# A fused attention and gated expert kernel: first h phase through the out-projection's banks, and a new order of early loads

## The chip, the cores and the metric

The kernel runs on one core of a Trainium2 chip. The metric is device time in microseconds for one execution, lower is better; the median over repeated runs is compared.

## The reference

Two stages are chained. The first attends twice in each of 8 batches and 8 heads, with 576 positions, head size 64 and 32 packed queries p:

```python
def sm_attn(qq, kk, vv):
    s = scale * np.matmul(qq, kk.transpose(0, 1, 3, 2))
    s = s - np.max(s, axis=-1, keepdims=True)
    a = np.exp(s)
    a = a / (np.sum(a, axis=-1, keepdims=True) + 1e-09)
    return np.matmul(a, vv)
p_packed = sm_attn(p, k, v)
out = sm_attn(q, p_packed, p_packed)
```

The second takes the result as 4608 tokens of 512 and computes, with 2048 inner columns:

```python
h = x @ w_in
g = h * np.cos(h)
return (g @ w_out).astype(np.float32)
```

Inputs and the output are float32.

## The kernel before, in words

Everything on chip is bfloat16 with float32 accumulation. The work goes batch by batch, each in these steps:

- `load` (L81) brings k, v or q of a batch from HBM and casts it on the way; it is a DMA issued by POOL (GpSimd). `load_w_in` and `load_w_out` bring each of the two weights in four blocks of 512 KB, also from POOL's queue.
- k and q are transposed, on TensorE (`pe_T`, L94, three groups of eight transposes, each group copied out of PSUM) or by a DMA transpose issued by SP (`xbar`, L90). v is rearranged by a copy, `permute_v` (L85), on DVE (VectorE) or POOL.
- `s1` (L128): scores of the packed queries against k, exponentials on ACT (ScalarE). The exponentials are transposed by `a1_pe` (TensorE) or `a1_xbar` (DMA). `pp` (L157) multiplies them with v and lays the result out as `ppT`.
- `ppw` (L174): instead of multiplying attention's output with w_in, the packed values are multiplied with w_in first, in four pieces n of 512 columns, giving `PPW`. Each piece is copied out of PSUM by DVE or ACT.
- `s2` (L185), `sums2` and `normalise`: scores of q against the packed values, exponentials, sums by a matmul with ones, a logarithm and a negative exponential on ACT, and the product `a2n` on DVE.
- h phase, 16 chunks `fc` of 128 inner columns: `h_mm` (L212) makes h in PSUM by four matmuls (L220), the cosine on ACT (L224), and the product `gT` on DVE (L227). Every eight chunks POOL copies the last 64 rows into `joint`, where two batches share one output chunk.
- out-projection: `out_gen` (L265) yields after each of 16 matmuls (L270) per chunk of 128 rows, then copies the result to `osb`, alternately by DVE and ACT, and writes it out from SP.

The order is written by hand: engines run their own instructions in program order. The out-projection of the previous batch is the filler: `fill(n)` (L287) puts n of its matmuls at the place where it stands, so that TensorE has work while another engine is waited for. `slot` (L394) runs an h phase with the remaining fillers spread over its chunks, and with inserted work at named chunks. `warm` puts dummy matmuls at the start. In the loop from L426 on, each batch has the same sequence: second attention of batch s, first attention of batch s+1 and DMA transposes for s+1, then the h phase of s.

PSUM is in two pools: `psA`, three tiles of two banks each (`psa`, L78), used by the h phase and by all attention steps, and `psO`, two single banks (`ot`), used by the out-projection and by the dummy matmuls. An h chunk holds its `psA` tile until DVE has made the product.

POOL's loads run in the order of issue. A small POOL copy into `gate` makes POOL wait for a DMA transpose before it issues the loads behind it. The ACT tables for exponentials and for the cosine are different; each change is a table load.

The first h phase (L356 to L361) has no filler, since no previous batch exists. After it come the first attention of batch 1 with the first batch's out-projection between its steps, then batch 2's first attention, and the h phase of batch 1 as a slot.

Of the kernel before, what the change touches and what calls it, by code (L numbers as in the profile page):

```python
# [8 lines left out]
FP32 = mybir.dt.float32  # L9
BF16 = mybir.dt.bfloat16  # L10
# [5 lines left out]
def kernel(  # L16
# [55 lines left out]
    def copy(eng, out, in_):  # L72
        if eng is ACT:
            ACT.copy(out=out, in_=in_)  # L74
        else:
            eng.tensor_copy(out=out, in_=in_)  # L76

    def psa(dt=FP32):  # L78
        return A.tile([128, 2, 512 if dt == FP32 else 1024], dt, name="psA", tag="A")

    def load(n, b):  # L81
        bf[n, b] = bf_pool.tile([TP, H, C * D], BF16, name=n + "bf", tag=n + "bf")
        G.dma_start(out=bf[n, b], in_=srcs[n][b].rearrange("h (p c) d -> p h (c d)", c=C))  # L83

    def permute_v(b, eng=G):  # L85
# [2 lines left out]
             bf["v", b].rearrange("p h (c d) -> p c h d", c=C))  # L88

    def xbar(n, b):  # L90
        t = xT[n, b] = att_pool.tile([128, H * 3, TP], BF16, name=n + "T", tag=n + "T")
        nc.sync.dma_start_transpose(out=t, in_=bf[n, b].rearrange("p h x -> p (h x)"))

    def pe_T(n, b, engs=(V, V, V)):  # L94
        t = xT[n, b] = att_pool.tile([128, H * 3, TP], BF16, name=n + "T", tag=n + "T")
        flat = bf[n, b].rearrange("p h x -> p (h x)")
        for i in range(3):
            ps = psa(BF16)
            for j in range(8):
                o = 8 * i + j  # L100
                nc.tensor.transpose(ps[:, 0, j * TP:(j + 1) * TP], flat[:, o * 128:(o + 1) * 128],  # L101
                                    ident[0:TP, 0:TP])
            copy(engs[i], t[:, 8 * i:8 * i + 8].rearrange("p a x -> p (a x)"),
                 ps[:, 0, 0:8 * TP])

    def pack_p(b0, b1):
        ng = 2 * (b1 - b0)
        ps = psa(BF16)
        flat = ps.rearrange("p a x -> p (a x)")
        for g in range(ng):  # L110
            nc.tensor.transpose(flat[:, g * 128:(g + 1) * 128],
                                p_bf[:, 2 * b0 + g].rearrange("p t d -> p (t d)"), ident)
        V.tensor_copy(out=P2[:, b0:b1].rearrange("p b h n -> p (b h n)"), in_=flat[:, 0:ng * 128])
# [32 lines left out]
        nc.sync.dma_start_transpose(out=t.rearrange("p a c x -> p (a c) x"),  # L146
                                    in_=a1[b % 2].rearrange("p a c x -> p (a c x)"))

    def a1_pe(b):
        t = a1T[b] = att_pool.tile([128, 2, C, 128], BF16, name="a1T", tag="a1T")  # L150
        for y in range(2):
            ps = psa(BF16)
            for c in range(C):
                nc.tensor.transpose(ps[0:TP, 0, c * 128:(c + 1) * 128], a1[b % 2][:, y, c, 0:TP], ident)
            copy(V, t[0:TP, y].rearrange("p c x -> p (c x)"), ps[0:TP, 0, 0:C * 128])
# [15 lines left out]
            z = slice(64 - 64 * y, 128 - 64 * y)  # L171
            ACT.copy(out=t[z, :, y, :], in_=pv[r, :, y, :])  # L172

    def ppw(b, n, eng=None):  # L174
        if b not in PPW:
            PPW[b] = ppw_pool.tile([128, 2, DF], BF16, name="PPW", tag="PPW")
        ps = psa()
        for x in range(4):
            for y in range(2):
                r = slice(64 * y, 64 * y + 64)  # L180
                nc.tensor.matmul(ps[32 * x:32 * x + 32, y, :], ppT[b % 2][r, 2 * x + y, :],  # L181
                                 w_in_bf[r, x, n * 512:(n + 1) * 512], start=True, stop=True)
        copy(eng or (V, ACT)[n % 2], PPW[b][:, :, n * 512:(n + 1) * 512], ps)

    def s2(b):  # L185
        a2u[b] = att_pool.tile([128, 2, S], BF16, name="a2u", tag="a2u")
# [63 lines left out]
    def n_chunks(b):  # L250
        return 5 if b % 2 and b < B - 1 else 4
# [11 lines left out]
                q.dma_start(out=rows[:, cols], in_=osb[a:z, cols])  # L263

    def out_gen(b):  # L265
        for c in range(n_chunks(b)):
            ps = O.tile([128, DM], FP32, name="ot", tag="ot")
            for fc in range(NFC):
                w = joint[b // 2][:, fc, :] if c == 4 else gT[b][:, fc, c * 128:(c + 1) * 128]
                nc.tensor.matmul(ps, w, w_out_bf[:, fc, :], start=(fc == 0), stop=(fc == NFC - 1))  # L270
                if fc < NFC - 1:
                    yield
            osb = o_pool.tile([128, DM], FP32, name="osb")
            copy((V, ACT)[n_out[0] % 2], osb, ps)
            n_out[0] += 1
            for a, z, rows in pieces_of(b, c):
                nc.sync.dma_start(out=rows, in_=osb[a:z, :])
            yield

    filler = [None, 0]  # L280

# [11 lines left out]
    def load_w_in(n):  # L293
        G.dma_start(out=w_in_bf[:, :, n * 512:(n + 1) * 512],
                    in_=moe_w_in.rearrange("(a p) n -> p a n", p=128)[:, :, n * 512:(n + 1) * 512])

    def load_w_out(n):
        G.dma_start(out=w_out_bf[:, n * 4:(n + 1) * 4, :],
                    in_=moe_w_out.rearrange("(a p) n -> p a n", p=128)[:, n * 4:(n + 1) * 4, :])

    def dup_p(a, b):
        for t in range(2):
            V.tensor_copy(out=p_bf[:, a:b, t, :], in_=p_raw[:, a:b, :])

    def warm(n):
        for _ in range(n):
            nc.tensor.matmul(wps, wz[:, 0:128], wz, start=True, stop=True)

# [2 lines left out]
    load("v", 0)  # L311
    make_identity(nc, ident)
    load("q", 0)
    load_w_in(0)
    load_w_in(1)
    G.dma_start(out=p_raw[:, 2:, :], in_=p_rows[:, 2:, :])
    load_w_in(2)
    load_w_in(3)
    for n in range(4):
        load_w_out(n)  # L320
    load("k", 1)
    load("v", 1)
    load("q", 1)
    load("k", 2)
    load("v", 2)
    load("q", 2)
    wz = const.tile([128, 512], BF16, name="wz")
    wps = O.tile([128, 512], FP32, name="wps", tag="ot")
    V.memset(wz, 0.0)
    ACT.preload_act_table_set(EXP_SET)  # L330
    V.memset(ones_blk, 0.0)
# [3 lines left out]
        V.memset(t[:, :, :, TP:128], 0.0)  # L335

    warm(7)
    dup_p(0, 2)
    pack_p(0, 1)
    warm(9)  # L340
    pe_T("k", 0, (V, ACT, V))
    s1(0)
    permute_v(0, V)
    warm(3)
    a1_pe(0)
    recips(0)
    pp(0)
    pe_T("q", 0, (V, ACT, V))
    s2(0)
    ppw(0, 0)  # L350
    sums2(0, 0)
    sums2(0, 1)
    normalise(0)
    warm(6)
    dup_p(2, 16)
    for fc in range(NFC):  # L356
        h_mm(0, fc)()
        if fc in (1, 4, 7):
            ppw(0, 1 + fc // 3)
        if fc == 10:  # L360
            pack_p(1, 3)  # L361

    set_filler(0)
    ACT.preload_act_table_set(EXP_SET)
    fill(4)
    pe_T("k", 1)
    fill(3)
    s1(1)
    permute_v(1, V)
    fill(8)  # L370
    a1_pe(1)
    recips(1)
    fill(4)
    pp(1)
    pe_T("q", 1)
    fill(3)
    ppw(1, 0)
    s2(1)
    fill(4)
    pe_T("k", 2)  # L380
    ppw(1, 1)
    fill(3)
    s1(2)
    fill(4)
    sums2(1, 0)
    fill(4)
    sums2(1, 1)
    normalise(1)
    fill(6)
    a1_pe(2)  # L390
    recips(2)
    load("k", 3)

    def slot(s, pieces, hooks, keep=5):  # L394
        left = filler[1] - keep
        for fc in range(NFC):
            rest = h_mm(s, fc)
            while pieces and pieces[0][0] == fc:
                pieces.pop(0)[1]()
            rest()  # L400
            while hooks and hooks[0][0] == fc:
                hooks.pop(0)[1]()
            done = left + keep - filler[1]
            fill((left * (fc + 1)) // NFC - done)

    def pw(b, n):
        return lambda: ppw(b, n)

    def pw2(b):
        fill(4)  # L410
        ppw(b, 0)
        ppw(b, 1)
        fill(4)

    def begin_loads(b):
        G.tensor_copy(out=gate, in_=xT["k", b][0:1, 0, 0:1])
        for n, i in (("v", b), ("q", b), ("k", b + 1)):
            load(n, i)

    permute_v(2)  # L420
    xbar("q", 2)
    xbar("k", 3)
    slot(1, [(1, pw(1, 2)), (4, pw(1, 3)), (7, lambda: pp(2)), (9, lambda: pack_p(3, B)),
             ], [(8, lambda: begin_loads(3)), (12, lambda: pw2(2))])

    for s in range(2, B):  # L426
        nxt = s + 1 < B
        fill(1000)
        set_filler(s - 1)
        ACT.preload_act_table_set(EXP_SET)  # L430
        if nxt:
            permute_v(s + 1)
        s2(s)
        ppw(s, 2, V)
        fill(8)
        if nxt:
            s1(s + 1)
            ppw(s, 3, V)
            xbar("q", s + 1)
            if s + 2 < B:  # L440
                xbar("k", s + 2)
            a1_xbar(s + 1)
            recips(s + 1)
            G.tensor_copy(out=gate, in_=a1T[s + 1][0:1, 0, 0, 0:1])  # L444
        else:
            ppw(s, 3, V)
        fill(4)
        sums2(s, 0)
        fill(5)
        sums2(s, 1)  # L450
        normalise(s)
        fill(13)
        for n, b in (("v", s + 2), ("q", s + 2), ("k", s + 3)):
            if b < B:
                load(n, b)
        pieces = [(5, lambda: pp(s + 1))] if nxt else []
        slot(s, pieces, [(9, lambda: pw2(s + 1))] if nxt else [])
    set_filler(B - 1)
    fill(1000)
    tail_chunk(B - 1, 4)  # L460
# [30 lines left out]
```

The softmax here doesn't subtract the row's maximum and nothing guards it: scores larger than these inputs give would overflow.

## Time and profile before

| What | Value |
| --- | --- |
| median of 13 runs | 261.31 us (261.01 to 262.49) |
| profiled execution, own time | 261.08 us |
| its span, first to last instruction | 259.3 us |
| PE busy | 238.4 us (92%), 2037 matmuls |
| DVE busy | 165.6 us (64%) |
| ACT busy | 166.6 us (64%) |
| POOL busy | 53.6 us (21%) |
| out-projection matmuls, `ot` from `w_out_bf` and `gT` | 512, 379 ns mean |
| h matmuls, `psA` from `a2n` and `PPW` | 512, 285 ns mean |
| h product on DVE | 128, 755 ns mean |
| cosine on ACT | 128, 651 ns mean |
| granted TensorE clock | 1.0 throughout |

PE is TensorE's matmul stream. Matmuls are pipelined, so the mean of one is a latency and more than the distance from one to the next. An engine's idle time costs nothing where another engine sets the pace, so the table is read by stage, with the chain that ended last and the waits. In a timeline row the columns are start and length in us, engine, line, operation, output and input, count, and in brackets the idle time before it and what ended it. In a table of stretches, each row has the stretch, its length, busy time and count of each engine in the order PE, weight load, DVE, ACT, POOL, then granted clock, mean DMA share and GB/s.

### The profile page before, as it was taken

How to read it: one execution, taken by the hardware profiler on the slowest of the kernel's cores; microseconds unless marked ns; L12 is line 12 of the kernel's file. 1: busy time of each engine (PE TensorE's matmuls, PEld its weight loads, DVE VectorE, ACT ScalarE, POOL GpSimd, SP SyncE). 2: the span in 40 equal slices, each digit the busy share in tenths (PEclk: the TensorE clock that was granted, in tenths of full speed). 3: DMA queues.
4: the chain of work that ended last, by engine and by line, in shares of the span. 5: the costliest groups of instructions: out<-in, count | busy, mean ns of one | idle time of the engine just before them, and what ended most of it. 6: DMA issues, size and time to landing. Idle time of an engine off the chain costs nothing.

```text
span 259.3 us, 5064 instructions
## 1 busy us (share of the span) xinstructions
PE 238.4 (92%) x2037; PEld 132.7 (51%) x2037; DVE 165.6 (64%) x253; ACT 166.6 (64%) x270; POOL 53.6 (21%) x67
## 2 busy tenths in 40 slices
PE   8876759998989999999999999999999999999993
PEld 3543426554644656455545654565446564565452
DVE  2558856749875587568866675578755875687110
ACT  1378762497687657787787667777786576884000
POOL 8523002430422030504050305020310000000000
PEclk9999999999999999999999999999999999999999
DMA  6999999999499999699959993979192111121232
GB/s 96 204 227 207 206 204 198 200 198 182 68 202 213 193 142 214 117 194 159 211 108 193 159 218 89 177 156 208 51 154 81 40 43 40 40 52 46 66 83 81
DMA packets 62919, 37.09 MB, mean 143 GB/s; under 512 B 35520, under 2 KB 58304, under 8 KB 62896
## 3 DMA queue, kind: packets, MB, share of 16 engines
q0 software_dynamic: 23168, 18.81, 47.6%
q1 hardware_dynamic: 39568, 17.83, 32.8%
q8 instruction: 16, 0.26, 0.4%
q10 hardware_dynamic: 160, 0.13, 0.2%
q14 instruction: 7, 0.06, 0.1%
HBM read 37.22 MB, written 9.44 MB: 180 GB/s over the span
## 4 chain that ended last, share of the span: by engine, by line
PE 72%; DMA 13%; ACT 7%; DVE 4%; issue 1%; POOL 1%; DVEq 0%; POOLq 0%; ACTq 0%
PE ot L270 43%; PE psA L220 19%; DMA kbf<-in_k_dram 7%; DMA w_in_bf<-in_moe_w_in_dram 5%; PE psA L181 3%; DVE gT L227 2%; PE psA L162 2%; ACT cosT L224 1%; PE ot L259 1%; PE psA L123 1%; PE psA L197 1%; ACT a2u L189 1%; PE psA L101 1%; ACT L430 1%; ACT PPW L74 1%
## 5 line engine op out<-in xcount | busy, mean ns | idle before, releaser
L270 PE MATMUL ot<-w_out_bf,gT 128*128 128x512 bf16 x512 | 131.8, 379 | 0.0
L227 DVE TENSOR_TENSOR gT<-psA,cosT 128x576 bf16<-128x576 f32 x128 | 93.8, 755 | 28.6 <-ACT cosT L224 27.1
L224 ACT ACTIVATE cosT<-psA 128x576 bf16<-128x576 f32 x128 | 81.5, 651 | 30.2 <-PE psA L220 27.5
L220 PE MATMUL psA<-a2n,PPW 128*128 128x288 bf16 x512 | 81.2, 285 | 6.8 <-DVE gT L227 3.5
L270 PEld LDWEIGHTS <-gT 128*128 128x128 bf16 x512 | 47.9, 98 | 44.6 <-issue 7.4
L220 PEld LDWEIGHTS <-PPW 128*128 128x128 bf16 x512 | 49.9, 97 | 39.7 <-issue 12.4
L76 DVE CAST PPW<-psA 128x1024 bf16<-128x1024 f32 x22 | 26.9, 1221 | 11.8 <-PE psA L181 11.8
L231 POOL COPY joint<-gT 128x512 bf16<-128x512 bf16 x16 | 9.7, 612 | 103.4 <-DVE gT L227 103.4
L76 DVE COPY osb<-ot 128x512 f32<-128x512 f32 (+1 forms) x19 | 12.8, 673 | 17.6 <-PE ot L270 14.1
L207 DVE SCALAR_TENSOR_TENSOR a2n<-a2u,r,lns 128x576 bf16<-128x576 bf16 x16 | 12.4, 816 | 16.0 <-ACT lns L205 16.0
L74 ACT COPY osb<-ot 128x512 f32<-128x512 f32 (+1 forms) x18 | 10.4, 575 | 17.9 <-PE ot L270 13.2
L76 POOL COPY vp<-vbf 96x3072 bf16<-96x3072 bf16 x6 | 16.5, 2746 | 0.1
L132 ACT ACTIVATE a<-psA 128x576 bf16<-128x576 f32 x16 | 10.2, 648 | 7.0 <-PE psA L123 7.0
L199 ACT ACTIVATE lns<-psA 128x576 f32<-128x576 f32 x16 | 10.4, 653 | 5.7 <-PE psA L197 5.2
L74 ACT CAST PPW<-psA 128x1024 bf16<-128x1024 f32 x10 | 10.1, 1012 | 5.5 <-PE psA L181 5.5
L181 PE MATMUL psA<-w_in_bf,ppT 64*32 64x512 bf16 x256 | 11.9, 381 | 1.3 <-DVE gT L227 0.9
L189 ACT ACTIVATE a2u<-psA,rs 128x576 bf16<-128x576 f32 x16 | 11.0, 736 | 2.6 <-PE psA L123 2.4
L270 PE MATMUL ot<-w_out_bf,joint 128*128 128x512 bf16 x48 | 12.3, 379 | 0.0
L172 ACT CAST ppT<-psA 64x128 bf16<-64x128 f32 x16 | 4.2, 260 | 11.2 <-PE psA L101 6.4
L83 POOL DMA_DIRECT2D kbf<-in_k_dram x8 | 6.3, 786 | 20.9 <-PE psA L101 17.2
L224 ACT ACT_TABLE_LOAD x8 | 10.3, 1283 | 0.1
L444 POOL COPY gate<-a1T 1x1 bf16<-1x1 bf16 x5 | 0.9, 179 | 45.4 <-DMA a1T<-a 45.4
(54 smaller groups left out, 150.7 us busy)
## 6 DMA issues: line engine op xcount, KB each, us to landing
kbf<-in_k_dram POOLq DMA_DIRECT2D x8, 576.0 KB, 11.4
vbf<-in_v_dram POOLq DMA_DIRECT2D x8, 576.0 KB, 6.7
qbf<-in_q_dram POOLq DMA_DIRECT2D x8, 576.0 KB, 9.3
out_dram<-osb SPq DMA_DIRECT2D x24, 192.0 KB, 2.7
out_dram<-osb SPq DMA_DIRECT2D x22, 128.0 KB, 2.4
w_in_bf<-in_moe_w_in_dram POOLq DMA_DIRECT2D x4, 512.0 KB, 15.1
w_out_bf<-in_moe_w_out_dram POOLq DMA_DIRECT2D x4, 512.0 KB, 20.0
out_dram<-osb SPq DMA_DIRECT2D x26, 64.0 KB, 2.1
```

What stands on the lines that cost most here:

```text
L74: ACT.copy(out=out, in_=in_)
L76: eng.tensor_copy(out=out, in_=in_)
L132: ACT.activation(out=a1[b % 2][:, y, :, 0:TP].rearrange("p (e m) x -> p e m x", e=2), in_=ps[y][:, :, 0:HS].rearrange("p e (m x) -> p e m ...
L181: nc.tensor.matmul(ps[32 * x:32 * x + 32, y, :], ppT[b % 2][r, 2 * x + y, :], w_in_bf[r, x, n * 512:(n + 1) * 512], start=True, stop=True)
L189: ACT.activation(out=a2u[b][:, y].rearrange("p (e x) -> p e x", e=2), in_=ps[y][:, :, 0:HS], func=AF.Exp, scale=rs1[b][:, y:y + 1])
L199: ACT.activation(out=lns[b][:, y].rearrange("p (e x) -> p e x", e=2), in_=ps[:, :, 0:HS], func=AF.Ln)
L207: V.scalar_tensor_tensor(out=a2n[b][:, y], in0=a2u[b][:, y], scalar=r1[b][:, y:y + 1], in1=lns[b][:, y], op0=ALU.mult, op1=ALU.mult)
L220: nc.tensor.matmul(ps[:, e, 0:HS], PPW[b][:, y, fc * 128:(fc + 1) * 128], a2n[b][:, y, e * HS:(e + 1) * HS], start=(y == 0), stop=(y == 1))
L224: ACT.activation(out=csv, in_=ps[:, :, 0:HS], func=AF.Sin, bias=PI_HALF)
L227: V.tensor_tensor(out=gT[b][:, fc, :].rearrange("p (e x) -> p e x", e=2), in0=ps[:, :, 0:HS], in1=csv, op=ALU.mult)
L231: G.tensor_copy(out=joint[b // 2][:, fc - 7:fc + 1, j0:j0 + 64], in_=gT[b][:, fc - 7:fc + 1, 512:576])
L270: nc.tensor.matmul(ps, w, w_out_bf[:, fc, :], start=(fc == 0), stop=(fc == NFC - 1))
```

## The change

It has four parts.

First h phase: `ppw` pieces 1 to 3 of batch 0, the packing of p for batches 1 and 2, and k1's transposes on TensorE take `psO` banks (`bank`) instead of `psA` tiles. Piece 1 is computed ahead of the phase and copied after `normalise`; pieces 2 and 3 are copied half by ACT, half by DVE. k1's three transposes go in at chunks 9, 10 and 11. From chunk 12 on two out-projection matmuls of batch 0 follow each chunk; the first two output chunks of that batch are accumulated side by side, four inner chunks at a time, so that matmuls need only those h chunks, and the w_out blocks, that are there.

Loads: p's bulk after all of w_in, then k1, half of w_out, v1, q1, the other half of w_out, k2. The duplication of p for batches 1 to 7 and the rearrangement of v1 move from DVE to POOL. k's loaded tile and transposed tile get two buffers each.

Batches 1 and 2: k2 is transposed by DMA instead of TensorE. The three DMA transposes of k2, q2 and k3 stand together in SP's queue after `s2(1)`; v2 and q3 are loaded behind a gate on the last of them. `s1(2)`, `a1_pe(2)`, `pp(2)` and `ppw(2, 0..1)` leave the stretch before and in the h phase of batch 1, and stand after it, with `s1(3)` and a DMA transpose of its exponentials, in a sequence of their own for batch 2.

Later phases: in `slot`, inserted work always follows the chunk's product (`pp` stood between cosine and product before), and the fillers are spread by weights, with half of a heavy chunk's ahead of its insert.

The core of the diff:

```diff
-        bf[n, b] = bf_pool.tile([TP, H, C * D], BF16, name=n + "bf", tag=n + "bf")
+        bf[n, b] = bf_pool.tile([TP, H, C * D], BF16, name=n + "bf", tag=n + "bf", bufs=2 if n == "k" else 1)
...
-    def pe_T(n, b, engs=(V, V, V)):
+    def pe_T(n, b, engs=(V, V, V), groups=(0, 1, 2), own=False):
...
+            ps = bank(BF16) if own else psa(BF16)[:, 0, :]
...
+    def bank(dt=FP32):
+        return O.tile([128, 512 if dt == FP32 else 1024], dt, name="ot", tag="ot")
...
+        if own:
+            ps = [bank(), bank()]
+        else:
+            t = psa()
+            ps = [t[:, 0, :], t[:, 1, :]]
...
+            if own or two:
+                for y in range(2):
+                    copy(eng[y] if two else eng, PPW[b][:, y, n * 512:(n + 1) * 512], ps[y])
...
+        groups = [(0, 1), (2,), (3,)] if b == 0 else [(c,) for c in range(n_chunks(b))]
+        for grp in groups:
+            pss = {c: O.tile([128, DM], FP32, name="ot", tag="ot") for c in grp}
+            for f0 in range(0, NFC, 4):
+                for c in grp:
+                    for fc in range(f0, f0 + 4):
...
-    load_w_in(0)
-    load_w_in(1)
+    for n in range(4):
+        load_w_in(n)
     G.dma_start(out=p_raw[:, 2:, :], in_=p_rows[:, 2:, :])
-    load_w_in(2)
-    load_w_in(3)
-    for n in range(4):
-        load_w_out(n)
     load("k", 1)
-    load("v", 1)
-    load("q", 1)
-    load("k", 2)
-    load("v", 2)
-    load("q", 2)
...
     permute_v(0, V)
+    load_w_out(0)
+    load_w_out(1)
+    load("v", 1)
...
     pe_T("q", 0, (V, ACT, V))
+    load("q", 1)
+    load_w_out(2)
+    load_w_out(3)
+    dup_p(2, 16, G)
+    load("k", 2)
+    permute_v(1, G)
...
+    warm(6)
+    rest_ppw = ppw(0, 1, V, own=True, later=True)
     normalise(0)
-    warm(6)
-    dup_p(2, 16)
+    rest_ppw()
+    set_filler(0)
     for fc in range(NFC):
         h_mm(0, fc)()
-        if fc in (1, 4, 7):
-            ppw(0, 1 + fc // 3)
-        if fc == 10:
-            pack_p(1, 3)
...
+        if fc in (3, 6):
+            ppw(0, 2 + fc // 6, (ACT, V), own=True)
+        if fc == 7:
+            pack_p(1, 3, bank(BF16))
+        if fc in (9, 10, 11):
+            pe_T("k", 1, (V, ACT, V), (fc - 9,), own=True)
+        if fc >= 12:
+            fill(2)
+
+    def slot(s, hooks, keep=0, heavy={}):
+        left = filler[1] - keep
+        weight = [1 + heavy.get(fc, 0) for fc in range(NFC)]
+        for fc in range(NFC):
+            h_mm(s, fc)()
+            quota = (left * sum(weight[:fc + 1])) // sum(weight) - (left + keep - filler[1])
+            first = quota
+            while hooks and hooks[0][0] == fc:
+                if first == quota and fc in heavy:
+                    first = quota // 2
+                    fill(first)
+                hooks.pop(0)[1]()
+            fill(quota - first if first != quota else quota)
...
     ACT.preload_act_table_set(EXP_SET)
+    s1(1)
     fill(4)
+    pe_T("q", 1)
+    load("q", 2)
+    load("k", 3)
+    fill(2)
+    a1_pe(1, (0,))
+    fill(2)
+    a1_pe(1, (1,))
+    recips(1)
     fill(3)
+    pp(1)
+    fill(5)
+    s2(1)
+    ppw(1, 0, V)
+    xbar("k", 2)
+    xbar("q", 2)
+    xbar("k", 3)
+    G.tensor_copy(out=gate, in_=xT["k", 3][0:1, 0, 0:1])
+    load("v", 2)
+    load("q", 3)
     fill(4)
+    ppw(1, 1, V)
     sums2(1, 0)
     sums2(1, 1)
     normalise(1)
+    fill(11)
+    slot(1, [(3, lambda: pw2(1, 2, (ACT, V))), (6, lambda: pack_p(3, B)),
+             (8, lambda: (permute_v(2), load("v", 3), load("k", 4)))], 4)
+
+    fill(1000)
+    set_filler(1)
+    ACT.preload_act_table_set(EXP_SET)
+    s1(2)
+    fill(9)
+    a1_pe(2, (0,))
+    fill(3)
+    a1_pe(2, (1,))
+    recips(2)
+    permute_v(3)
+    fill(3)
+    s1(3)
+    pp(2)
+    a1_xbar(3)
+    recips(3)
     fill(6)
+    s2(2)
+    ppw(2, 0, V)
+    xbar("q", 3)
+    xbar("k", 4)
+    fill(4)
+    sums2(2, 0)
+    ppw(2, 1, V)
+    sums2(2, 1)
+    normalise(2)
+    fill(8)
+    G.tensor_copy(out=gate, in_=xT["k", 4][0:1, 0, 0:1])
+    for n, b in (("v", 4), ("q", 4), ("k", 5)):
+        load(n, b)
+    fill(8)
+    slot(2, [(3, lambda: pw2(2, 2, (ACT, V))), (7, lambda: pp(3)), (11, lambda: pw2(3))], 5, {11: 3})
+
+    for s in range(3, B):
...
-        pieces = [(5, lambda: pp(s + 1))] if nxt else []
-        slot(s, pieces, [(9, lambda: pw2(s + 1))] if nxt else [])
+        slot(s, [(5, lambda: pp(s + 1)), (10, lambda: pw2(s + 1))] if nxt else [], 5, {10: 3})
```

## The prediction

> **What bounds the kernel now.** I read the busy shares by slice, then the chain that ended last, then a table of busy times by stage, then each engine's timeline up to 90 us.
>
> From the page, 40 slices of 6.48 us:
>
> ```profile
> PE   8876759998989999999999999999999999999993
> DVE  2558856749875587568866675578755875687110
> DMA  6999999999499999699959993979192111121232
> ```
>
> PE is solid from about slice 12 (76 us). What can be won lies before. There, DMA stands at 9 tenths and PE at 5 to 9. The chain in order of time (start, length, what) names the early limit:
>
> ```profile
> 5.00 14.00 DMA w_in_bf<-in_moe_w_in_dram
> 19.05 0.53 issue
> 19.58 19.21 DMA kbf<-in_k_dram
> 38.83 1.19 PE psA L101 x24
> ```
>
> All of w_out and the rest of w_in land ahead of k1. The same by stage (h0 ends at 36.2, attention 1 and its fillers to 57.2, h1 to 75.4, then the next attention and h2):
>
> ```profile
> 36.20:38.83 2.63, 0.00 (x0) 0.00 (x1) 0.46 (x1) 0.97 (x1) 0.00 (x0) 1.00 1.31 203
> 38.83:57.20 18.37, 17.24 (x229) 10.22 (x230) 10.73 (x21) 9.47 (x19) 6.98 (x7) 1.00 1.26 199
> 57.20:75.40 18.20, 16.45 (x157) 9.57 (x157) 16.11 (x26) 13.19 (x22) 2.97 (x5) 1.00 0.92 146
> 84.30:103.20 18.90, 18.90 (x150) 11.36 (x149) 13.36 (x20) 12.75 (x22) 3.09 (x5) 1.00 1.07 188
> ```
>
> Second number: length; then PE, weight load, DVE, ACT, POOL. PE lies dead for 2.6 us before k1. In h1 DVE is the full engine (16.1 of 18.2), and in h2 it is PE.
>
> Landings, from who waited for them: w_in block 1 at 19.05, large p 20.8, k1 38.8, v1 41.7:
>
> ```profile
> 20.80 1.16 DVE L303 CAST p_bf<-p_raw 128x896 bf16<-128x896 f32 x2 [0.26 <-DMA p_raw<-in_p_dram]
> 41.71 0.96 DVE L76 COPY vp<-vbf 96x3072 bf16<-96x3072 bf16 x1 [0.84 <-DMA vbf<-in_v_dram]
> 19.58 0.79 POOL L83 DMA_DIRECT2D kbf<-in_k_dram  x1 [2.85 <-DMA w_in_bf<-in_moe_w_in_dram]
> ```
>
> k1 to v1 gives 2.9 us per q/k/v load, and from p to k1, (38.8-20.8-2.9)/6 = 2.53 us per half-megabyte weight block; p took 1.75. The third line and those around it show POOL's loads issued in order, each waiting for the one eight places earlier to land.
>
> **What the Trainium skill says.** "DMA: Bandwidth & Descriptors", section "Issuing engines are not separate DMA queues": transfers from all issuing engines share 16 engines. The trace agrees: over 50 to 61 us, with loads and transposes together, 190 GB/s, against 205 for loads alone. So order of issue decides what is late. "GPSIMD Engine Reference", section 3.1: at best about 1.8 cycles per element at 1.2 GHz; its two casts of 896 columns would be 1.34 us each (an estimate by that page). The trace's POOL copies (612 ns for 512, 2746 for 3072) give 0.8 to 1.1 us instead. No POOL cast from float32 is shown.
>
> **The change part by part.**
>
> *Loads.* After w_in 1 (19.05) now come w_in 2, 3, p, k1, w_out 0, 1, v1, q1, w_out 2, 3, k2. Adding the durations above: w_in 3 at 24.1, p 25.9, k1 28.7, w_out 0 31.3, w_out 1 33.8, v1 36.6, q1 39.5, w_out 2 42.0, w_out 3 44.5, k2 47.4. k1 comes 10 us earlier. q1, until now at 38.8+2x2.9 = 44.6, comes 5.1 us earlier (two weight blocks fewer ahead).
>
> *h0.* DVE's list after 21.9 (before: two p casts of 1.16 precede; after: the PPW piece, two copies of about 0.66) is 16 products of 0.74, two PPW halves of 0.66, one P copy 0.41, two k1 copies 0.56: 14.7 us, to 36.6, as now (36.7). Now 14.0 busy out of 16.3 has gaps, since inserts take one of three product banks; those gaps close, and are spent on k1's transposes and 8 out-projection matmuls (about 0.2 each). POOL's p casts begin at 25.9 and end at 27.9 to 28.6; PE reaches the P transposes at about 26.7 and stalls. DVE is covered to 28.2, so the loss is 0 to 0.5. A late h0 has cover up to about 2 us, for PE then waits for q1. With two banks of their own, each insert waits for the copy of the one two before; those copies are queued right behind the product of the same chunk, so I cost the wait at nothing. batch 1's permute moves from DVE (0.96) to POOL (2.75): v1 at 36.6, done at 39.4, wanted by pp at 42.8; the joint copies and q2's and k3's issues behind it are wanted later than that.
>
> *Attention 1.* PE does scores(1) (two free banks at 35.7) and 4 fillers by 36.8, then waits for q1 until 39.5: the 2.7 us stall moves from k1 to q1. Then q1's transposes 1.0, 4 fillers and 12 a1 transposes, to 42.1; fillers on w_out 2 (42.0) 42.8; pp to 43.5; ppT copies on DVE 0.6 and ACT 0.53 to 44.6; s2 scores and ACT exponentials 1.4 to 46.5; sums, two Ln 1.3, two Exp 1.25 to 49.3; products on DVE to 50.4; table load 1.28 done by 51.2 (a c1 copy of 0.6 is ahead of it). First cosine 51.4, now 57.67: 6.3 us earlier. Now, this stage also held k2's transposes 1.0, s1(2) 0.26, a1(2) 0.7, and 43 fillers against 39 so far.
>
> *h1.* Out go pp(2), two PPW pieces of batch 2 and their copies; in come 5 more fillers. I take 0.8 per product with 21 fillers (12.8), two split PPW 1.4, P 0.8, an output copy 0.5: 15.5 us. Last product ends at 51.4+0.65+15.5 = 67.5, now 76.06: 8.5 earlier. Owed to later by PE: s1(2) 0.26, a1 0.7, pp 0.7, two PPW pieces 0.56, less one filler: 2.0. So 6.5 us net.
>
> *Attention 2, rebuilt.* s1(2) 67.0, 9 fillers, a wait of 0.45 for the exponentials behind the c3 copy and table load, a1 and s1(3) to 71.7, pp to 72.4, s2 at 73.8, sums to 76.1, 16 fillers to 79.5, when the normalised tiles are ready. h2 starts at 79.5, now 84.1: 4.6, plus 11 more fillers done (2.4), less two PPW pieces left (0.56): 6.4, consistent.
>
> *k2, q2, k3 as a group.* Transposes now follow each other on SP like this, with the gate's end:
>
> ```profile
> 77.78 3.64 SPq L92 DMA_TRANSPOSE qT<-qbf  x1
> 81.59 2.90 SPq L92 DMA_TRANSPOSE kT<-kbf  x1
> 84.54 1.93 SPq L146 DMA_TRANSPOSE a1T<-a  x1
> 89.43 0.18 POOL L444 COPY gate<-a1T 1x1 bf16<-1x1 bf16 x1 [10.02 <-DMA a1T<-a]
> ```
>
> The k2 transpose starts at 47.5, q2's load is in by about 52, k3's by 56; three transposes of 3.6 and 5 to landing end near 62. All three are needed at 67, 73.8 and 71.4: hidden. Batch 0's output writes queue behind them on SP; four output buffers cover it. Behind the gate on POOL stand v2 and q3: v2 issued at 62.5, in by 68 to 69 (5.7 to 6.7 to landing), its permute 2.75 to about 71.5; pp(2) wants it at 71.7. No cover is left; everything on PE queues behind pp(2). I charge 0.5 us (0 to 3). v3's permute (about 80) is wanted at 87.
>
> *h2.* PE work: 7.8+34 fillers 7.3+pp 0.7+four PPW 1.1 = 17.0; DVE 16.3. The PPW pair at chunk 3 takes two of three banks with only 2 fillers as cover. I charge 1.1 us of gaps (0.3 to 2); h2 now has none.
>
> *h3 and on.* pp no longer sits between a cosine and its product (waits of 0.7 in three places), and fillers are spread round the PPW pair (a 0.55 gap in each short stage, as at 126.5). Worth 0.6 us (0 to 1.2). The tail is unchanged.
>
> **Sum.** 6.4-0.5-1.1+0.6 = 5.4 us. Profiled span 259.3 goes to 253.9, its own time 261.08 (1.8 around the span) to 255.7. The median 261.31 is 0.2 above that execution: I say 255.8.
>
> **Rivals.**
> *Partly given back* (257.2 to 260.5): bank gaps in h1 and h2 twice as large and v2 2 us late, 5.4-3.0 = 2.4 saved, 258.9. For it: h1 now loses 1.75 us of PE time to gaps. Against: its inserts are lighter.
> *More* (252.5 to 254.3): h2 without gaps, v2 in time, spread fillers at their best: 5.4+0.5+1.1+0.6 = 7.6, 253.7.
> *Slower, by v2's chain*: v2 is loaded only after k3 is transposed. If transposes among loads run at half speed (7 us each instead of 3.6), the gate opens at 72, v2 is in at 79, permuted at 81.7, and pp(2) waits 10 us: 5.9-10 = 4 us slower, 265. It decides once v2 lands after about 74.5. For it: transposes and loads share engines, and landing here took up to 6.7 where SP had been busy 3.9. Against: q2's transpose at 56.1 took 3.94 with k3's load in flight.
> *No change*: each early gain only waits for a later load; DMA at 9 tenths speaks for it. Against: from 76 us on no PE wait names a DMA.
>
> **How the numbers follow.** Main case 0.62 (254.3 to 257.2 by its own bounds), partly given back 0.17, more 0.09, no change 0.03, slower 0.09. A measurement here tells 0.2% (0.5 us) from nothing. Faster: 0.62+0.17+0.09 = 0.88. The range 253.5 to 259.4 leaves out the slower and unchanged cases and the ends of the two neighbours: 0.2.
>
> **What would show it.** k1's transposes inside h0 near 29 us, a PE wait for q1 until 39.5, first h1 cosine at 51 to 52, last h1 product at 67 to 68, first h2 cosine near 80, POOL's gate near 62, pp(2) with at most 1 us of wait. It is wrong if q1 lands after 41 (loads slower than 2.9 and 2.53 us), if pp(2) waits long for v2, or if DVE cannot hold 0.8 us per product with own banks.

## The result, and the profile after

The changed kernel takes 258.72 us (median of 11 runs, 257.81 to 260.46) against 261.31; the ratio, which is not the quotient of these medians, is 0.9895, 95% interval 0.9871 to 0.9919. Ratios leave out executions more than 1.5% above the fastest of the same kernel, which below concerns only the kernel with q1 ahead of v1 (five of eleven). So 2.6 us were gained where 5.5 were forecast. The forecast was wrong in size: under half of it came, and the time lies in the case that was called "partly given back" (257.2 to 260.5, chance 0.17).

The page of the changed kernel, slices of 6.45 us, with the granted TensorE clock in tenths:

```profile
PE   8877687989979999999999999999999999999993
DVE  2549874679657777577856775579657764786110
PEclk9999997999999999999999999999999999999999
```

Counted from 0, PE is weak before slice 13 in slices 2 to 4 (4 holds a wait for p's casts), 6 and 11, and slice 6 has a clock of 0.7, which the kernel before did not show in its profile. The chain that ended last, in order of time:

```profile
19.63 20.53 DMA qbf<-in_q_dram
40.16 0.05 issue
40.21 1.23 PE psA L103 x16
...
73.08 0.56 DVE a1T L76
73.64 0.08 DVE r L146
73.72 0.02 issue
73.75 1.86 DVE rs L147
75.61 0.02 issue
75.63 0.87 PE psA L169 x24
```

The early load on the chain is now q1, as forecast, and a second stop appears at 73.75, ahead of pp(2): `rs`, on DVE, takes 1.86 us. pp(2) does not read `rs`; what it reads is v2's rearranged copy, which ended at the same moment (below). h0, h1 and so on are the h phases of batches 0, 1 and on. The stages that answer to those of before (wait for the load, attention 1, h1, h2), columns as there:

```profile
37.90:40.20 2.30, 0.15 (x1) 0.00 (x0) 0.00 (x0) 1.62 (x5) 2.30 (x2) 1.00 1.25 206
40.20:53.10 12.90, 12.50 (x125) 7.05 (x126) 8.10 (x14) 5.25 (x10) 2.51 (x4) 0.87 1.30 198
53.10:68.20 15.10, 14.50 (x111) 9.07 (x111) 13.09 (x19) 12.02 (x19) 2.33 (x4) 1.00 0.96 173
83.60:101.80 18.20, 17.59 (x155) 10.47 (x154) 13.77 (x21) 12.82 (x23) 5.35 (x6) 1.00 1.09 189
```

Attention 1 ran at a mean clock of 0.87. In three stretches of 1 us (the third column from the end is the clock: 1.00, 0.50, 1.00), TensorE was idle just before the halved stretch, which lasts from 40.5 to 43.9:

```profile
39.00:40.00 1.00, 0.00 (x0) 0.00 (x0) 0.00 (x0) 0.53 (x2) 1.00 (x1) 1.00 1.25 209
41.00:42.00 1.00, 0.99 (x14) 0.86 (x12) 0.92 (x2) 0.00 (x0) 0.17 (x1) 0.50 1.25 204
44.00:45.00 1.00, 1.00 (x11) 0.67 (x10) 0.63 (x2) 0.00 (x0) 0.07 (x1) 1.00 1.30 203
```

POOL's timeline shows the landings, p at 27.0, v1 at 37.3, and the group's gate with what stands behind it:

```profile
26.99 1.81 POOL L327 CAST p_bf<-p_raw 128x896 bf16<-128x896 f32 x2 [1.67 <-DMA p_raw<-in_p_dram]
37.32 2.74 POOL L76 COPY vp<-vbf 96x3072 bf16<-96x3072 bf16 x1 [7.78 <-DMA vbf<-in_v_dram]
...
64.30 0.18 POOL L433 COPY gate<-kT 1x1 bf16<-1x1 bf16 x1 [20.23 <-DMA kT<-kbf]
64.81 0.77 POOL L83 DMA_DIRECT2D vbf<-in_v_dram  x1 [0.33 <-POOL gate L433]
...
72.83 2.74 POOL L76 COPY vp<-vbf 96x3072 bf16<-96x3072 bf16 x1 [5.87 <-DMA vbf<-in_v_dram]
```

v2 was issued at 64.8 and landed at 72.8; its permute ended at 75.6, and pp(2) began at 75.6. By place in the span:

| Place | before | forecast | changed |
| --- | --- | --- | --- |
| q1 can be transposed | 44.6 (estimate) | 39.5 | 40.2 |
| first h1 cosine | 57.67 | 51.4 | 53.85 |
| last h1 product ends | 76.06 | 67.5 | 68.98 |
| first h2 matmul | 84.12 | 79.5 | 83.59 |
| first matmul of s2(3) | 104.27 | 99.5 (104.27-4.8, from the sum) | 103.15 |
| end of the span | 259.3 | 253.9 | 258.1 |

This execution took 260.15, 1.4 above the median, and only 0.9 under the profiled one of before. So its timeline explains a gain of 0.9 us; the other executions have no trace.

### The profile page after: what moved, and what is told of

Read it like the earlier page. It is cut to its first block, busy times and chain, and to the rows that moved or that the text cites. A ratio compares the mean times of both kernels' runs of the same rounds, so it can differ in the third digit from the quotient of the medians.

```text
span 258.1 us, 5022 instructions
## 1 busy us (share of the span) xinstructions
PE 238.5 (92%) x2013; PEld 132.2 (51%) x2013; DVE 165.0 (64%) x252; ACT 166.4 (64%) x272; POOL 58.2 (23%) x70
## 4 chain that ended last, share of the span: by engine, by line
PE 68%; DMA 13%; ACT 9%; DVE 5%; issue 2%; POOL 1%; DVEq 0%; ACTq 0%; POOLq 0%
PE ot L294 40%; PE psA L241 17%; DMA qbf<-in_q_dram 12%; DVE gT L248 4%; PE psA L193 3%; ACT cosT L245 2%; ACT a2u L210 2%; PE psA L169 2%; PE psA L218 1%; DMA a1T<-a 1%; PE ot L280 1%; PE psA L128 1%; ACT L481 1%; PE psA L103 1%; ACT osb L74 1%
## 5 line engine op out<-in xcount | busy, mean ns | idle before, releaser
L294 PE MATMUL ot<-w_out_bf,gT 128*128 128x512 bf16 x512 | 134.6, 381 | 0.0
L241 PE MATMUL psA<-a2n,PPW 128*128 128x288 bf16 x512 | 83.3, 286 | 3.4 <-DVE gT L248 2.1
L76 DVE CAST PPW<-psA 128x1024 bf16<-128x1024 f32 (+1 forms) x24 | 27.0, 1133 | 11.4 <-PE psA L193 11.4
L252 POOL COPY joint<-gT 128x512 bf16<-128x512 bf16 x16 | 9.8, 613 | 79.5 <-DVE gT L248 79.5
L76 POOL COPY vp<-vbf 96x3072 bf16<-96x3072 bf16 x7 | 19.2, 2747 | 18.7 <-DMA vbf<-in_v_dram 18.7
L193 PE MATMUL psA<-w_in_bf,ppT 64*32 64x512 bf16 x232 | 10.8, 381 | 0.9 <-DVE gT L248 0.5
L226 ACT ACTIVATE lns<-lns 128x576 f32<-128x576 f32 x16 | 10.0, 678 | 0.0
L332 PE MATMUL ot<-wz 128*128 128x512 bf16 x25 | 8.6, 497 | 1.2 <-DVE wz L344 1.2
L74 ACT CAST PPW<-psA 128x1024 bf16<-128x1024 f32 (+1 forms) x9 | 7.3, 821 | 3.2 <-PE psA L193 3.2
```

Source lines behind the costliest of these rows:

```text
L193: nc.tensor.matmul(ps[y][32 * x:32 * x + 32, :], ppT[b % 2][r, 2 * x + y, :], w_in_bf[r, x, n * 512:(n + 1) * 512], start=True, stop=True)
L226: ACT.activation(out=lns[b][:, y], in_=lns[b][:, y], func=AF.Exp, scale=-1.0)
L241: nc.tensor.matmul(ps[:, e, 0:HS], PPW[b][:, y, fc * 128:(fc + 1) * 128], a2n[b][:, y, e * HS:(e + 1) * HS], start=(y == 0), stop=(y == 1))
L294: nc.tensor.matmul(pss[c], w, w_out_bf[:, fc, :], start=(fc == 0), stop=(fc == NFC - 1))
```

## The experiments

Theory A: two loads are late, q1 and v2, each stops TensorE, and each stop is paid in full at the end, since TensorE is full afterwards. The rival, theory B: the pace of DVE and ACT in the h phases sets the end. All runs were timed beside the kernel before; ratios are to it, and the changed kernel stands at 0.9895. The executions of the kernel before fall in two groups, near 261.2 and 262.5 us, so that its median moved between 261.31 and 262.48 from one set of runs to the next; ratios of different sets are therefore compared with care. The dummy matmuls' results are not used.

**Keep TensorE busy while it waits for q1.**

```diff
     fill(4)
+    wps = psa()
+    for _ in range(10):
+        nc.tensor.matmul(wps[:, 0, :], wz[:, 0:128], wz, start=True, stop=True)
     pe_T("q", 1)
```

> Ten dummy matmuls (2.1 us, into a product tile that nothing reads) stand on TensorE ahead of q1's transposes, so that it isn't idle while it waits for q1. Theory A (the late q1 costs twice: the wait, and a clock halved from 40.2 to 43.6 because TensorE had been idle; PE is full afterwards, so all of it reaches the end): granted clock 1.0 there, q1's 24 transposes in 1.0 us instead of 2.0, first h1 cosine 1.7 us earlier, near 52.1, and 1.5 us off the end: ratio to the kernel before about 0.983. Theory B (the pace of DVE and ACT in the h phases sets the end, earlier starts are absorbed): cosine earlier, ratio unchanged at 0.989. A third, that the clock has nothing to do with the idle time: clock still 0.5 there, no change.

Measured: 258.07 us, ratio 0.984 (0.981 to 0.9871). The transposes of q1 in the changed kernel's TensorE timeline, then in this one's (start, length, in brackets the wait):

```profile
40.21 2.03 PE L103 MATMUL psA<-ident,qbf 96*128 96x96 bf16 x24 [2.15 <-DMA qbf<-in_q_dram]
```

```profile
41.10 1.19 PE L103 MATMUL psA<-ident,qbf 96*128 96x96 bf16 x24
```

The dummies end after q1 has landed, and still the h1 phase starts 0.85 earlier (51.55 against 52.40): from the start of q1's transposes to pp(1) it is 3.4 us instead of 5.1. The median of six executions is 0.65 us lower, not 1.5, and the intervals touch. In this profile the clock was lowered earlier, in the first h phase, after another wait of 2.2 us there, for p's casts on POOL. At h2 this execution is 1.9 us ahead of the changed kernel's. Of this the dummies can have given 0.85. The other 1.0 came at pp(2), whose wait for v2 was 0.54 instead of 1.56 because k3's transpose landed, and the gate opened, at 62.9 instead of 64.3.

**q1 ahead of v1; v2 ahead of k3; both.** The first:

```diff
     load_w_out(1)
-    load("v", 1)
...
     load("q", 1)
+    load("v", 1)
```

> q1 is loaded ahead of v1, everything else as in the changed kernel. Theory A: q1 in at 37.3 instead of 40.2, no wait of 2.2 us and no halved clock; v1 comes 2.9 us later, its permute ends near 43.2, and pp(1) may wait up to 1 us for it. First h1 cosine at 51.3 to 51.8 (now 53.85), ratio about 0.981. Theory B: cosine earlier, ratio unchanged at 0.989.

The second:

```diff
     load("q", 2)
+    load("v", 2)
     load("k", 3)
...
     G.tensor_copy(out=gate, in_=xT["k", 3][0:1, 0, 0:1])
-    load("v", 2)
     load("q", 3)
```

> v2 is loaded ahead of k3 and so not behind the gate on k3's transpose; q3 stays behind it. Theory A: v2 in before 57, its permute done before the h1 phase ends, pp(2) without its wait of 1.6 us; k3's load and transpose 3 us later, at about 67, still ahead of s1(3) at 73.6. h2 starts about 1.6 us earlier, ratio about 0.984. Theory B: ratio unchanged at 0.989. The rival that the load among the transposes delays k2's transpose: s1(2) waits for it at 68.7.

Both edits in one kernel:

> Both: q1 ahead of v1, and v2 ahead of k3. Theory A: the two gains add, 3.5 to 4 us under the changed kernel, ratio 0.975, about 254.8. Theory B: no more than 0.987.

Measured: 0.9899 (0.9858 to 0.994), 0.9882 (0.9849 to 0.9915), and 0.9841 (0.9806 to 0.9876, 258.22 us). q1 alone gained nothing: the median of all its eleven executions is 260.87 us, and they spread from 257.56 to 263.11. Its profile is of the slowest, so it shows what can happen and not what is usual. There h1 started 1.0 earlier, at 51.4, but the stop moved to v2, which came no earlier:

```profile
75.94 1.46 PE L169 MATMUL psA<-a1T,vp 96*128 96x64 bf16 x24 [2.90 <-POOL vp L76]
```

After this wait of 2.9 us the clock was lowered (mean 0.88 from 70 to 84), so that pp(2) took 1.46 instead of 0.87. With v2 ahead of k3 the wait for v2 is gone, and s1(2) did not wait for k2's transpose (it ran at 67.55), so the rival named for this run is out. But another stop came in v2's place. DVE's timeline and POOL's, at the same moment:

```profile
78.78 4.03 DVE L228 SCALAR_TENSOR_TENSOR a2n<-a2u,r,lns 128x576 bf16<-128x576 bf16 x2 [0.35 <-ACT lns L226]
```

```profile
79.12 3.08 POOL L76 COPY vp<-vbf 96x3072 bf16<-96x3072 bf16 x1 [6.65 <-PE ot L294]
```

The two products of normalise(2) take 1.55 us elsewhere. Here POOL permuted v3 while DVE read two tensors from SBUF, and the second product ended 0.6 after POOL's copy. TensorE waited 1.7 us for it. In the profile of both edits together (256.71 us, its fastest execution) the permute began at 79.38, as the second product was ending (79.70). In that execution, which has neither stop, theory A's 3.5 to 4 us are nearly there: the first matmul of s2(3) comes at 99.71, 3.4 ahead of the changed kernel's. In the median they are not (258.22 against 258.72): the sum assumed that no new stop takes a removed one's place. Which stop the other five executions had is not shown.

**POOL's permutes out of the way.** As both edits, with this on top:

```diff
+    load_w_in(0)
+    load_w_in(1)
     G.dma_start(out=p_raw[:, 2:, :], in_=p_rows[:, 2:, :])
+    load_w_in(2)
+    load_w_in(3)
...
     load("k", 3)
+    permute_v(2)
+    load("v", 3)
...
-             (8, lambda: (permute_v(2), load("v", 3), load("k", 4)))], 4)
+             (8, lambda: (permute_v(3), load("k", 4)))], 4)
...
     recips(2)
-    permute_v(3)
```

> As e4_both, and on POOL: v2's permute and v3's load stand right behind k3's load, ahead of the gate, v3's permute in the h1 phase, and p's bulk is loaded ahead of w_in blocks 2 and 3 again. Theory C (a POOL copy that runs while DVE reads two SBUF tensors holds DVE up: in e3_v2_ahead the two products of the normalisation took 4.03 us instead of 1.55 while v3's permute ran): those products take 1.55 in every execution, h2 starts near 80, all executions near e4_both's best: 256.7, ratio 0.979; TensorE doesn't wait 2 us for p's casts. The rival, that the spread of e4_both comes from the clock alone: ratio stays at 0.984 and the products were never long.

Measured: 256.93 us, ratio 0.9803 (0.9766 to 0.9841). The ratio is the one of theory C. The products took 1.55 in the profile, and the wait for p's casts was gone. The executions are not all near 256.7, as expected: they spread from 255.77 to 258.52, the two slowest with the two lowest clocks (0.987 and 0.99, the others 0.997 or more). In the profile, one of these two, a wait of 2.2 us for w_out block 2 ended at 42.28, with a lowered clock after it.

The same theory by itself, on the kernel with v2 ahead of k3:

```diff
     recips(2)
-    permute_v(3)
...
     normalise(2)
+    G.tensor_copy(out=gate, in_=a2n[2][0:1, 1, 0:1])
+    permute_v(3)
```

> As e3_v2_ahead, with v3's permute on POOL held until the second product of normalise(2) is written (a one-element POOL copy reads it). Theory C (a POOL copy holds up DVE where DVE reads two SBUF tensors): the two products take 1.55 us in place of 4.03, h2's second half-chunk starts 1.7 us earlier, ratio 0.982 instead of 0.988. The rival, that the products were long for a reason of their own: still 4 us, ratio 0.988.

Measured: 257.9 us, ratio 0.983 (0.9783 to 0.9877), as the theory had it, though the interval overlaps that of the kernel without the hold (0.9849 to 0.9915). The lines say it more plainly; from h2's first matmul to s2(3) it is 19.6 us, against 21.4 without the hold:

```profile
80.15 1.55 DVE L228 SCALAR_TENSOR_TENSOR a2n<-a2u,r,lns 128x576 bf16<-128x576 bf16 x2 [0.35 <-ACT lns L226]
```

```profile
81.76 0.18 POOL L469 COPY gate<-a2n 1x1 bf16<-1x1 bf16 x1 [9.43 <-DVE a2n L228]
81.88 2.74 POOL L76 COPY vp<-vbf 96x3072 bf16<-96x3072 bf16 x1
```

**v1's permute on DVE again**, on top of the POOL order:

```diff
-    permute_v(1, G)
...
     recips(1)
-    fill(3)
+    permute_v(1, V)
...
     pp(1)
-    fill(5)
+    fill(8)
```

(The loads and the permute that follow q2's load in the code move behind this permute, in the same order on POOL.)

> As e5_pool_order, with v1's permute on DVE again (0.96 us instead of 2.74 on POOL) and pp(1) ahead of the three out-projection matmuls that need w_out block 2. e5 waited 2.2 us for that block, and its clock was halved afterwards. Theory A: v1 in at 39.8, pp(1) near 41, first h1 matmul near 49.5 (51.4 in e5, 52.4 in the changed kernel), ratio about 0.974. Theory B (the h phases set the end): ratio stays at 0.980.

Measured: 256.58 us, ratio 0.9785 (0.9744 to 0.9827). The first h1 matmul came at 49.23, as expected; the ratio lies between the two values expected, and its interval holds both. The wait that is left in attention 1, on PE, and a new stop in attention 2, on DVE:

```profile
41.68 0.87 PE L169 MATMUL psA<-a1T,vp 96*128 96x64 bf16 x24 [1.78 <-DVE vp L76]
```

```profile
70.58 2.08 DVE L147 TENSOR_SCALAR rs<-r 128x2 f32<-128x2 f32 x1
```

POOL rearranged v3 from 69.88 to 72.63, and `rs`, 0.17 us elsewhere, ended with it. h1 begins 2.2 us earlier than in e5_pool_order, h2 only 1.4 earlier. This version has the lowest median, 5.0 us under the kernel before (261.56 beside it). But its interval overlaps that of e5_pool_order (0.9766 to 0.9841), so the last edit's own gain is not shown.

Between theories A and B the traces decide better than the ratios. In the changed kernel and in its eight variants, the h1 phase lasts 16.6 us from its first matmul to its last product, whether it starts at 49.2 or at 52.6. From the first matmul of s2(3) to the end of the span it is 154.9 to 155.1 us in twelve of the thirteen profiles, the kernel before among them; the exception is e5_pool_order (156.1), whose clock was halved in its last 2 us. So an early start is not absorbed by the h phases, as theory B had it: what TensorE loses or gains ahead of these places reaches the end. Theory A was right in this and wrong in the sums, because new stops appeared.

**The clock by itself.** The kernel before waits 2.8 us for k1. Its executions fall in groups, mostly 261.2 and 262.5 us, so a test of the clock can stand on it:

```diff
     fill(4)
+    dum = psa()
+    for _ in range(12):
+        nc.tensor.matmul(dum[:, 0, :], wz[:, 0:128], wz, start=True, stop=True)
     pe_T("k", 1)
```

> The kernel before, with twelve dummy matmuls (2.6 us, into a product tile that nothing reads) ahead of k1's transposes, where TensorE waits 2.8 us. Clock theory (a long wait of TensorE halves its clock for one stretch, in some executions, and that is the 1.2 us between executions of 261.2 and 262.5): nearly all executions fall at 261.2 with a clock of 0.997 or more, ratio 0.996 to 0.998. The rival, that the two groups have another cause: two groups as before, ratio 1.000.

Measured: 261.3 us, ratio 0.9967 (0.9949 to 0.9985). Of its 22 executions 21 lie between 261.1 and 261.8 and the last at 262.17; of the 27 of the kernel before beside it, 13 lie above 262.3, all with a clock of 0.993 or less, while the nine with 1.0 took 261.2 to 261.6. The times fit. The clocks fit less well: 15 of the 22 have 0.997 or more, and the other seven, down to 0.987, took 261.15 to 262.17, so a lowered clock in some other place cost them little.

**Parts of the change alone.** The new insertion order and filler weights, on the kernel before, from batch 3 on:

```diff
-        slot(s, pieces, [(9, lambda: pw2(s + 1))] if nxt else [])
+        slot_new(s, [(5, lambda: pp(s + 1)), (10, lambda: both(s + 1))] if nxt else [], 5, {10: 3})
```

(`slot_new` is the changed `slot`; `both` is two `ppw`.)

> The kernel before with the new insertion order and filler weights in the h phases from batch 3 on, nothing else. The prediction's step: 0.6 us less (0 to 1.2), ratio 0.998, with no waits for ppT or in the short stages. The rival: TensorE's fillers are only moved, ratio 1.000.

Measured: ratio 1.0 (0.9978 to 1.0021). The interval just takes in the 0.998 expected; the trace leaves nothing of it, since from s2(3) to the end it is 155.0 us, as in the kernel before. k1 ahead of w_out, on the kernel before:

```diff
+    load("k", 1)
     for n in range(4):
         load_w_out(n)
-    load("k", 1)
```

> The kernel before with k1's load ahead of all of w_out, nothing else. If q1's arrival sets the pace (theory of the prediction): k1's wait of 2.8 us goes, but q1 stays at 44.6, so at most 0.7 us is gained, ratio 0.997 to 1.000. If k1's wait was itself the loss: 2.8 us, ratio 0.989, and this alone would be the change's whole gain.

Measured: 261.38 us, ratio 0.9954 (0.9933 to 0.9975): 1.2 us, between the two. k1's wait went, as both had it, but less than half of its 2.8 us came off. Its profile is one of the executions with a lowered clock and took 261.65; the six that kept a clock of 1.0 took 260.06 to 260.53, about 1.1 under those of the kernel before (261.10 to 261.44). In the profile the next load, v1, is late in k1's place: its copy on DVE began at 41.68, the moment it had landed, the evictions of a1T stand behind that copy, and TensorE waited for them. Then it took up q1 at 44.6, where the estimate had put it. DVE's timeline and TensorE's:

```profile
41.68 0.96 DVE L76 COPY vp<-vbf 96x3072 bf16<-96x3072 bf16 x1 [3.58 <-DMA vbf<-in_v_dram]
42.55 1.01 DVE L76 COPY a1T<-psA 96x768 bf16<-96x768 bf16 x2
```

```profile
43.62 0.86 PE L162 MATMUL psA<-a1T,vp 96*128 96x64 bf16 x24 [1.69 <-DVE a1T L76]
```

The first h phase with its inserts back in product tiles (the rest of the change as it is):

```diff
-    rest_ppw = ppw(0, 1, V, own=True, later=True)
+    rest_ppw = ppw(0, 1, V, later=True)
...
-            ppw(0, 2 + fc // 6, (ACT, V), own=True)
+            ppw(0, 2 + fc // 6, (ACT, V))
...
-            pack_p(1, 3, bank(BF16))
+            pack_p(1, 3)
...
-            pe_T("k", 1, (V, ACT, V), (fc - 9,), own=True)
+            pe_T("k", 1, (V, ACT, V), (fc - 9,))
```

> The changed kernel with the first h phase's inserts (PPW pieces 1 to 3, p, k1's transposes) back in product tiles, everything else as changed. Prediction's step: h0 ends 1 to 2 us later and the wait for q1 shrinks by as much, so the ratio stays at 0.989 to 0.991. The rival, that the banks carry the gain: ratio 0.996 or more.

Measured: 258.96 us, ratio 0.9859 (0.9826 to 0.9893), so no loss against the banks is seen. Its h0 matmuls end at 37.24, 1.1 later, and the wait for q1 shrank by 1.0:

```profile
40.27 0.85 PE L103 MATMUL psA<-ident,qbf 96*128 96x96 bf16 x16 [1.13 <-DMA qbf<-in_q_dram]
```

So the banks named first in the change carry none of its gain here, because the next load is later than either version of h0. In this profile the h1 phase even starts 1.2 us earlier than in the changed kernel's (51.20 for 52.40): q1's transposes begin at the same time, but after the shorter wait the clock stayed at 1.0. Later it loses this again, since v3's rearranging on POOL held up the products of normalise(2) as in e3_v2_ahead (4.12 us).

## Why the prediction was wrong in size, by its own steps

- **Loads.** Right in order, 0.7 us late: q1 at 40.2 for 39.5, v1 at 37.3 for 36.6, p at 27.0 for 25.9. As the Trainium skill says in "DMA: Bandwidth & Descriptors", section "Issuing engines are not separate DMA queues", transfers share the engines; the trace agrees: 206 GB/s with loads alone (37.9 to 40.2), and 198 in the stretch after it, where a transpose joins them. The durations taken from the profile of before were about right for this stretch.
- **h0.** Right: it ended at 37.6 where 36.6 was forecast, and this cost nothing, since q1 was awaited. The casts on POOL took 1.81 us for the pair, within what the trace's copies gave (0.8 to 1.1 each) and under the 1.34 each estimated from the skill's page, but p was late, and the P transposes waited 1.9 us. This wait passed without a lowered clock.
- **Attention 1.** This step failed in size: the first h1 cosine came at 53.85, 2.45 later than forecast. 0.7 is q1's landing. From q1's first transpose to pp(1) were 5.1 us, where the step counted 3.3. In e3_v2_ahead and e8_psa_inserts, where q1's transposes also begin at 40.3 but at full clock, it is 3.8 us, and h1 starts at 51.2 instead of 52.4. e11_permute_held, the same program as e3_v2_ahead up to there, had its clock halved at this place and started h1 at 52.6. So about 1.2 us are the halved clock, and 0.5 the step had undercounted. (With the dummies ahead it is 3.4; there q1 had landed 0.9 before its transposes began.) The step priced a TensorE wait by its length and put what follows it at nothing. The skill has this in "TensorE: Matmul & The Clock Gate", section "Part 1: The HAM clock gate (the "warmup" mystery)": an idle window of about 3.4 us lowers the clock to half until TensorE has been busy for about as long. The halved stretch here was 3.4 us long, 40.5 to 43.9; the wait ahead of it was shorter than the page's window, 2.15 us.
- **h1.** 15.1 us from first cosine to last product, where 16.15 was taken: 1.0 better.
- **k2, q2, k3 as a group, and v2.** The step that failed most against what it charged. The order was right and the danger was named, but 0.5 us was charged and 1.6 paid. The gate opened at 64.3 for 62. k2's transpose held SP for 6.11 us, not 3.6, and k3's, begun at 57.75, took 6.6 us until the gate opened, not 5:

```profile
48.24 6.11 SPq L92 DMA_TRANSPOSE kT<-kbf  x1
54.52 3.13 SPq L92 DMA_TRANSPOSE qT<-qbf  x1
57.75 2.98 SPq L92 DMA_TRANSPOSE kT<-kbf  x1
60.79 9.45 SPq L301 DMA_DIRECT2D out_dram<-osb  x8
```

  In e1_dummies k2's transpose held SP as long (6.14), but k3's, begun at 57.69, took 5.2 to the gate, and pp(2) waited only 0.54. Why k3's took longer here stays open. And v2 took 8.0 us from issue to landing, not 5.7 to 6.7. Batch 0's output writes had piled up behind the transposes on SP and ran from 60.8 on, beside v2. That they cost v2 the difference was not tried separately.
- **Attention 2.** The step's count of TensorE's own work was 0.7 short: with no wait there it takes 13.2 us from s1(2) to h2 (66.92 to 80.15 in the run with both edits), and 12.5 was taken. Together with v2, h2 started at 83.59 instead of 79.5.
- **h2.** Right: 19.6 us from its first matmul to s2(3), where 18.1 and the five remaining fillers gave 19.2.
- **h3 and on.** Wrong: 0.6 forecast, nothing measured with that part alone. From s2(3) to the end the changed kernel takes 154.97 us, the kernel before 155.03.

In sum, from the forecast 4.8 us at s2(3) go 0.7 (q1), 1.2 (clock), 0.5 (attention 1's own count), 1.1 (v2) and 0.7 (attention 2), and 1.0 comes back in h1: 1.6 are left, and 1.1 were seen. Later 0.6 were missing. This is the account of the profiled execution, 0.9 us faster than that of before. The median gained 2.6; which of these losses the faster executions were spared was not traced. Of the rivals, "partly given back" gave the right time in part by luck: v2 was late as it said, but the gaps in h1 and h2 were 0.6 us each, not larger than forecast (1.1 in h2). The slower rival had v2's chain right, but only the first of its three transposes was slow, and pp(2) waited 1.6 us, not 10.

Shown by a run are the clock's part, v2's part (its wait goes when the load is moved), the banks' and the later phases' nothing, and the new stop between POOL and DVE. What stays open is how much of the spread of the changed kernel's executions (257.8 to 260.5) is the clock and how much POOL's permutes and v2's landing; its profile shows all of them in one execution. The mean clock alone does not sort its executions: the fastest and the slowest both have 0.987. v2's stop, in the four profiles with v2 behind the gate, ranged from 0.54 to 2.90 us.

## What to carry to other kernels

When a load is brought forward, follow the next one that TensorE needs, and the one after: here each removed wait handed on to the next load or to a copy engine, and some 5 us came only when q1, v2, p and POOL's permutes had all been moved. Price a TensorE wait of some 2 us with the slow stretch that may follow it (1.2 us here), not by its length alone. Before giving work better buffers, ask what the next stage waits for: if it is a load, the buffers buy nothing.

## What the runs showed of the hardware

- TensorE's granted clock fell to 0.50 for 3.4 us after a wait of 2.15 us (changed kernel, from 40.5 on); likewise after waits of 2.2 us (e1_dummies, in h0), 2.9 us (e2_q1_first, at 75.7), and 1.7 us (e7_k1_alone, 45.8 to 49.2). The profiled executions of the kernel before and of e6_slots_alone waited 2.8 and 3.3 us and kept 1.00. So waits shorter than the 3.4 us of the skill's page sufficed here, but not every time.
- The clock records say more on when. In all eight traces with a halved stretch in the middle, it begins a whole number of intervals of 3.413 us after the trace's first record (7 intervals in e1_dummies, 10 in the changed kernel, 21 in e2_q1_first). Cut into these intervals, the changed kernel's wait lies whole in one (37.1 to 40.5), while the kernel before's 2.8 us are split into 1.3 and 1.5, and those of e6_slots_alone into 1.8 and 1.6. Ahead of 250 us, all seven intervals in which TensorE was idle for 2.0 us or more (2.01 to 2.65) were followed by a halved one; of those below (up to 1.93) one was, with 1.66, in e7_k1_alone. That the idle time within an interval decides is read from this and was not tested; the one exception speaks against an exact limit.
- A POOL copy of 96x3072 held DVE up: two products with both inputs in SBUF took 4.03 us beside it and 1.55 without, and a 128x2 tensor_scalar on DVE (`rs`) took 1.85 instead of 0.17 while POOL permuted (changed kernel, at 73.75). In the five profiles where `rs` met such a copy it ended 0.02 to 0.03 us after the copy; the reciprocal of the same size just before it kept its 0.15 beside the copy. "GPSIMD Engine Reference", section 1 ("Specifications"), says that POOL shares its SBUF interfaces with DVE and contends with instructions that read two SBUF inputs or run in a two-port mode; the trace agrees and gives the size. That `rs` ran in such a mode is not shown. Products of an h chunk, which read PSUM and SBUF, kept their 0.74 us beside such copies: three took 2.17 at 57.90 in e5_pool_order, partly under a permute from 55.8 to 58.6.
